# Gate and up of a gated feed-forward block: rows stationary, 512 weight columns moving, results staged in pairs and turned by transfers

## The chip, the cores and the metric

The kernel runs on one core of one Trainium2 chip. The metric is device time in microseconds for one execution. "Before" has three runs: 1088.67, 1089.22 and 1090.31 us, median 1089.22. A separate execution was profiled.

## The reference

One transformer block on x of 2048 rows by 1024 columns, bf16: a layer norm, attention with 32 query heads that share one key head and one value head of width 32, a residual, a second layer norm, and a feed-forward of width 3584 whose gate is a sigmoid.

```python
q = (x @ wq).reshape(B, S, H, Dh)            # 32 heads of 32
k = x @ wk; v = x @ wv                       # one head of 32
scores = einsum("bhqd,bkd->bhqk", q, k) * (Dh ** -0.5)
o = einsum("bhqk,bkd->bhqd", softmax(scores), v)
h = x + (o reshaped to S x 1024) @ wo        # x in the products above is layernorm(x)
g, u = layernorm(h) @ w_gate, layernorm(h) @ w_up      # 1024 -> 3584
h2 = h + (sigmoid(g) * u) @ w_down                     # 3584 -> 1024
```

## The kernel before

The 2048 rows are 16 row tiles of 128 (t); two tiles are a unit, 8 units in all (UNITS). Attention works in 512 *bursts*. A burst is 128 keys against 128 rows of one tile and 16 heads: four matmuls of 32 contraction rows side by side (s_burst, L871, out S_ps), then two exponentials on ACT of 128x1024 (one_exp, L891, mostly into the ring Pr). A tile has 32 bursts. DVE adds pairs of exponentials for the row sums (L928, L940). PE multiplies them by V (pv_group, L978) and by ones (sum_group, L1025 and L1040), DVE normalises (L1083), and the attention output takes the place of the queries in QT. Then follow the output product with wo (wo_group), the second norm (stats2), and a transfer that transposes the normalised rows of the tile into QT again (transpose2, L623).

The feed-forward of a unit follows. gate_group and up_group compute 512 results a row per PSUM bank in the same helper (mm, L373; L375 where a matmul is issued in four narrow pieces of 32 output columns, so that it has the form of the PV product beside it). Weights are the stationary operand: 128 of their columns, with the transposed rows of the unit moving past them, 256 of them, or 128 where only the first tile of the unit is ready. So the result stands with the feed-forward width on partitions, as the down product needs it. ACT makes a tanh of the gate (L1305, into gu; the sigmoid is half of tanh plus one), DVE multiplies (L1327, into hact), and down_group reads hact as its stationary operand and writes rows out (L1365, then a transfer).

Weights of gate and up come in loads of 512 KB, 128 partitions x 8 x 256 columns (load_halves), issued on SP's queue into slots: four in wgu, the parts of QT that finished units leave free, and at the end the ring Pr. SP's queue also carries x, the outputs and the transposing transfers. Where a unit's second tile is not ready, its first runs alone (first_tile), and the weights of that step are loaded again for the second unless they are held.

The order of everything is fixed when the program is built. A planner keeps a clock for each engine and a price for each kind of work (T_MM, T_EXP, a price for changing the form of matmul, the rate of transfers) and deals the instructions out: a burst when its PSUM banks should be free, otherwise PV work by PV_PLAN, otherwise products of queries, wo, gate, up or down that its clocks say are ready (halves_ready, rows_ready). A PE with nothing ready gets dummy matmuls (fill, L409).

Of the kernel before, what the change touches and what calls it, by code (L numbers as in the profile page):

```python
# [7 lines left out]
BF16 = mybir.dt.bfloat16  # L8
# [78 lines left out]
def bass_sequential_preLN__grouped_kv_mqa__glu_gated_glu__prompt_kernel(  # L87
# [32 lines left out]
    U_PLAN = "75601517"  # L120
    PV_PLAN = "bbabdaaaEabeEaBadddabaEaAaaABaBabBaBbaEaaBAAaBabaaaBaDaaabaDabaabaEedEEa"
    WO_PLAN = "aababaaa"
    PV_HOLD = 0
    BANK_WAIT = 0.1
    NPB = 4
    G_SUM, HCH, HB0 = 4, 4, 2
    LN_LEAD = 4
    LN_RATE = 0.35
    T_PLAN = "aaaddadd"
    H_ROOM = 0.2  # L130
    Q_PLAN = "dadddddddddaddddddddddaddddddddd"
    SUM_PLAN = "ppppdddp"
    HOLD0 = 2
    K_BUSY = 10
    TODO = ["v5", "Q2", "q1b", "q1a", "k2", "v3", "q1d", "q0c", "C1", "v0", "C3", "v6", "v2", "v4", "C2", "v7",
            "k3", "v1", "q0d", "k1", "q1c"]
# [17 lines left out]
    WD_FROM, WD_GAP, WD_LATE = 30, 6, 14  # L154
    WD_GAP2 = 1
    TURN = 2
# [3 lines left out]
    QREC = 24  # L160
    QORD = 0
    URG0 = 0
    K_ACT = 3
    T_MM, T_FIX, T_SW, T_EXP, T_TANH, T_ADD = 0.0004167, 0.00267, 0.0995, 0.91, 0.479, 0.61
# [4 lines left out]
    with ExitStack() as es:  # L169
# [6 lines left out]
        QT = sb("QT", [NQ, S])  # L176
# [42 lines left out]
        d_sl = [ctr(f"d_sl{i}") for i in range(25)]  # L219
        block = EC(nc.Block())  # L220
# [37 lines left out]
        halves += [QT[:, :, c[0] * P:(c[1] + 1) * P] for c in UNITS[:-1]]  # L258
# [10 lines left out]
        def _(unused):  # L269
            sp, pe, act, dve, pool = nc.sync, nc.tensor, nc.scalar, nc.vector, nc.gpsimd  # L270

            def dma(q, dst, src, c, kb=256):
                q.dma_start(dst, src).then_inc(c.sem, 16)
                c.n += 16
                begin = max(CLK[id(q)][0], k_dma[0])
                k_dma[0] = begin + kb / (140.0 if q is pool else 275.0)
                c.at[c.n] = k_dma[0] + 1.15 + kb * 0.0037
                return (c, c.n)
# [77 lines left out]
            I_US, I_MAX = 4.0, 180  # L356
# [203 lines left out]
            def pe_transpose(t):  # L560

                need(pe, xn_val[t], ident_val)
# [181 lines left out]
            def q_tile(t, qs, on_act=False):  # L744
                items, n = [], len(qs)
                for h, q in enumerate(qs):
                    items += mm_list([(wq[:, q // 2, dt, q % 2 * P:(q % 2 + 1) * P], xnT[:, t // TPQ, dt, t % TPQ * P:(t % TPQ + 1) * P])
                                      for dt in range(DT)], lambda bank, h=h: bank[:, h * P:(h + 1) * P], P)

                def evac(bank, tick):  # L750
                    out = QT[:, qs[0]:qs[0] + n, t * P:(t + 1) * P]
# [11 lines left out]
                return _Group(items, evac, [wq_need(q) for q in qs] + xnT_ready(t))  # L763
# [8 lines left out]
            def q_group(q, c0, n):  # L772
                def evac(bank, tick):
# [5 lines left out]
                    out, src = QT[:, q, c0:c0 + n], bank[:, 0:n]  # L779
# [19 lines left out]
            def q_rows(g):  # L799
                t, i = ORDER[g]  # L800
                return QT[:, i // 2 * 4:i // 2 * 4 + 4, t * P:(t + 1) * P]

# [42 lines left out]
            def p_tile(k, h):  # L845
                kind, i = place[k]
                if kind == "Q":
                    c0 = (i + 4) * QC
                    return QT[:, 4 * h:4 * h + 4, c0:c0 + QC]
# [12 lines left out]
            def s_burst(k):  # L862
# [7 lines left out]
                for j in range(4):  # L870
                    ins = pe.matmul(S_ps[:, ((2 * k + j // 2) % 3) * 2 + j % 2, :],  # L871
                                    lhsT=kT4[DH * j:DH * (j + 1), kt * P:(kt + 1) * P],
                                    rhs=QT[DH * j:DH * (j + 1), i // 2 * 4:i // 2 * 4 + 4, t * P:(t + 1) * P],
# [94 lines left out]
            def pv_group(n):  # L968
# [3 lines left out]
                for b in bs:  # L972
                    def f2(bank, b=b):
# [7 lines left out]
                        if summed(g):  # L981
                            pv_done[0] = use(kx) + 1
                            return c_pv.inc(ins, 0.218, 0.17)
                        if b == bs[-1]:
                            return c_pe.inc(ins, 0.218, 0.17)
                        k_pe[0] += 0.218
                    items.append((0.218, f2, lambda k_=BURST_NO[g, b]: p_time(k_)))
# [17 lines left out]
            def sum_group(n):  # L1005
# [15 lines left out]
                def fs(bank):  # L1021
# [6 lines left out]
                    r = c_pe.inc(ins, 0.218, 0.17)  # L1028
# [4 lines left out]
                if not plain:  # L1033
                    items.append((0.218, fs, sum_time))
                alone = [BURST_NO[g, b] for b in bs] if plain else range(NB - 2, NB) if final else []
                for n, kx in enumerate(alone):
                    def fd(bank, n=n, kx=kx):
# [6 lines left out]
                        if plain:  # L1044
                            pv_done[0] = use(kx) + 1
                            return c_pv.inc(ins, 0.218, 0.17)
                        return c_pe.inc(ins, 0.218, 0.17)
                    items.append((0.218, fd, lambda kx=kx: p_time(kx)))

                def evac(bank, tick):  # L1050
                    if head and x % 2 == 0:
# [91 lines left out]
            down_last, gu_last = {}, {}  # L1143
            st2_val, h_done = {}, set()

            def wo_group(t, dc):
# [10 lines left out]
                items = mm_list([(QT[:, q, t * P:(t + 1) * P], wo[:, q, dc * 512:(dc + 1) * 512])  # L1157
# [623 lines left out]
```

## Time and profile before

| | us |
|---|---|
| median of the runs | 1089.22 (1088.67 to 1090.31) |
| the profiled execution's own time | 1089.49 |
| its span, first to last instruction | 1087.8 |
| PE busy | 1069.5 |
| ACT busy | 1001.9 |
| DVE busy | 896.4 |
| granted TensorE clock | 1.00 throughout |

A row of the page reads: line, engine, operation, out<-in by the program's names, shapes, count, then busy time and mean ns of one, then idle time of the engine before them and what ended it. Matmuls overlap, so a mean of 273 ns for one of 256 columns is its way through the array, and the time it costs is read from start to start. A row of the timeline merges like instructions: start, from the first start to the last end, and xN of them.

### The profile page before, as it was taken

To read this page: it belongs to the slowest core of one execution; us is meant where nothing else is said; L and a number is where in the kernel's file an instruction comes from. 1 tells how busy PE (TensorE), PEld (TensorE's weight loads), DVE (VectorE), ACT (ScalarE), POOL (GpSimd) and SP (SyncE) were. 2 spreads that over 40 slices of the span, in tenths; PEclk is the share of its full clock that TensorE was granted. 3 is DMA by queue.
4 is the path that set the end of the run, shared out by engine and by line. 5 is a ranking of instruction groups with operands and counts; after the bars stand their busy time and mean duration, and the time that the engine had idled before them with its cause. 6 is when DMAs were issued, how large, how long until landed. Compare 5 with 4: busy or idle time off the path is not lost.

```text
span 1087.8 us, 31948 instructions
## 1 busy us (share of the span) xinstructions
PE 1069.5 (98%) x13878; PEld 612.5 (56%) x13930; DVE 896.4 (82%) x1481; ACT 1001.9 (92%) x1151; POOL 64.0 (6%) x135
## 2 busy tenths in 40 slices
PE   8999999999999999999999999999999999999999
PEld 7433366544665456643666356653665447653884
DVE  7879898799798888888988988799988999798321
ACT  6999999999999999999999999999999999999110
POOL 2422110000000000000000000000000000000000
PEclk9999999999999999999999999999999999999999
DMA  8657338832977458770976619770686509771660
GB/s 199 132 123 213 90 111 231 240 89 70 230 206 169 117 138 226 213 188 26 248 203 182 136 32 276 196 179 26 158 227 185 126 22 261 203 191 41 152 175 20
DMA packets 320268, 169.98 MB, mean 156 GB/s; under 512 B 39424, under 2 KB 314112, under 8 KB 320128
## 3 DMA queue, kind: packets, MB, share of 16 engines
q1 hardware_dynamic: 315312, 158.23, 56.7%
q0 software_dynamic: 2592, 9.44, 2.6%
q8 instruction: 110, 1.80, 0.7%
q10 hardware_dynamic: 2224, 0.26, 0.2%
q14 instruction: 30, 0.25, 0.1%
HBM read 155.84 MB, written 4.19 MB: 147 GB/s over the span
## 4 chain that ended last, share of the span: by engine, by line
PE 66%; ACT 4%; issue 1%; DVE 1%; ACTq 0%
PE X_ps L373 40%; PE S_ps L871 10%; PE X_ps L375 8%; PE X_ps L978 7%; ACT Pr L891 3%; PE X_ps L1025 1%; ACT gu L1305 1%; DVE pairs L928 0%; DVE pairs L940 0%; DVE olp L994 0%; DVE hact L1327 0%; PE X_ps L1040 0%; DVE hx L1365 0%; ACTq L46 0%
## 5 line engine op out<-in xcount | busy, mean ns | idle before, releaser
L891 ACT ACTIVATE Pr<-S_ps 128x1024 bf16<-128x1024 f32 x992 | 941.1, 1181 | 0.4 <-PE S_ps L871 0.3
L928 DVE TENSOR_TENSOR pairs<-Pr 128x1024 bf16<-128x1024 bf16 x470 | 320.0, 682 | 27.4 <-ACT Pr L891 26.8
L940 DVE TENSOR_TENSOR pairs<-pairs 128x1024 bf16<-128x1024 bf16 x408 | 281.6, 690 | 12.0
L373 PE MATMUL X_ps<-QT,wgu 128*128 128x256 bf16 (+1 forms) x2235 | 215.7, 246 | 0.7 <-DMA QT<-hn 0.7
L871 PE MATMUL S_ps<-QT,kT 32*128 32x512 bf16 x2048 | 202.0, 385 | 2.4 <-ACT Pr L891 1.1
L373 PEld LDWEIGHTS X_ps<-QT,wgu 128*128 128x128 bf16 x2235 | 167.3, 98 | 40.6 <-issue 26.1
L373 PE MATMUL X_ps<-zone,hact 128*128 128x512 bf16 (+2 forms) x650 | 149.4, 371 | 4.4 <-issue 4.0
L373 PE MATMUL X_ps<-QT 128*128 128x128 bf16 (+1 forms) x1550 | 150.3, 246 | 0.0
L871 PEld LDWEIGHTS S_ps<-QT,kT 32*128 32x128 bf16 x2048 | 51.4, 91 | 156.9 <-ACT Pr L891 141.4
L373 PEld LDWEIGHTS X_ps<-QT 128*128 128x128 bf16 x1550 | 115.8, 98 | 25.1 <-issue 16.2
L978 PE MATMUL X_ps<-Pr,V 128*32 128x512 bf16 x1984 | 127.6, 381 | 0.4
L1305 ACT ACTIVATE gu<-X_ps 128x512 f32<-128x512 f32 x112 | 84.7, 756 | 45.8 <-PE X_ps L373 45.8
L1327 DVE SCALAR_TENSOR_TENSOR hact<-gu,X_ps 128x512 bf16<-128x512 f32 x112 | 76.6, 684 | 50.6 <-PE X_ps L373 47.0
L373 PEld LDWEIGHTS X_ps<-zone,hact 128*128 128x128 bf16 x685 | 59.1, 98 | 73.9 <-issue 18.6
L978 PEld LDWEIGHTS X_ps<-Pr,V 128*32 128x32 bf16 x1984 | 46.3, 96 | 51.8 <-issue 13.1
L375 PE MATMUL X_ps<-zone,hact 128*32 128x512 bf16 x956 | 61.9, 380 | 0.0
L464 POOL CAST mean<-mv 128x1 f32<-128x1 bf16 x28 | 7.6, 272 | 822.8 <-DVE mv L1191 791.1
L373 PE MATMUL X_ps<-wo,QT 128*128 128x512 bf16 x208 | 53.5, 380 | 1.3 <-issue 0.6
L373 PE MATMUL X_ps<-zone 128*128 128x128 bf16 (+3 forms) x461 | 49.8, 253 | 2.6 <-DMA zone<-hn 1.1
L375 PE MATMUL X_ps<-QT,wgu 128*32 128x256 bf16 (+1 forms) x1428 | 46.9, 265 | 0.9 <-DVE olp L994 0.9
L1365 DVE SCALAR_TENSOR_TENSOR hx<-X_ps,hx 128x512 bf16<-128x512 f32 (+2 forms) x33 | 22.2, 672 | 25.1 <-PE X_ps L373 23.0
L375 PEld LDWEIGHTS X_ps<-QT,wgu 128*32 128x32 bf16 x1428 | 33.2, 96 | 12.7 <-issue 7.5
(110 smaller groups left out, 631.7 us busy)
## 6 DMA issues: line engine op xcount, KB each, us to landing
wgu<-in_B_w_gate_dram SPq DMA_DIRECT2D x75, 512.0 KB, 5.3
wgu<-in_B_w_up_dram SPq DMA_DIRECT2D x74, 512.0 KB, 5.3
QT<-in_B_w_up_dram SPq DMA_DIRECT2D x49, 512.0 KB, 5.4
QT<-in_B_w_gate_dram SPq DMA_DIRECT2D x48, 512.0 KB, 5.7
zone<-in_B_w_down_dram POOLq DMA_DIRECT2D x14, 512.0 KB, 5.1
hx<-in_A_x_dram SPq DMA_DIRECT2D x17, 256.0 KB, 2.7
out_dram<-hx SPq DMA_DIRECT2D x31, 128.0 KB, 1.7
Pr<-in_B_w_gate_dram SPq DMA_DIRECT2D x5, 512.0 KB, 7.4
```

The costliest lines, as they stand in the source:

```text
L373: return pe.matmul(out, lhsT=lhsT, rhs=rhs, start=start, stop=stop, skip_group_check=main[0])
L375: ins = pe.matmul(out[DH * j:DH * (j + 1)], lhsT=lhsT[:, DH * j:DH * (j + 1)], rhs=rhs, start=start, stop=stop, tile_position=(0, DH * j), ...
L464: return c_pool.inc(pool.tensor_copy(out=mean[:, i:i + 1], in_=mv[:, i:i + 1, 0]), 0.2)
L871: ins = pe.matmul(S_ps[:, ((2 * k + j // 2) % 3) * 2 + j % 2, :], lhsT=kT4[DH * j:DH * (j + 1), kt * P:(kt + 1) * P], rhs=QT[DH * j:DH * ( ...
L891: c_e.inc(act.activation(out=p_tile(k, n % 2), in_=S_ps[:, 2 * pr:2 * pr + 2, :].rearrange("p a (b q) -> p (a b) q", q=QC), func=ACTF.Exp, ...
L928: slot_use[x] = c_dve.inc(dve.tensor_tensor(out=dst(x), in0=p_tile(k - 1, hh), in1=p_tile(k, hh), op=ALU.add), T_ADD, 0.08)
L940: slot_use[x] = slot_use[y] = c_dve.inc(dve.tensor_tensor(out=pairs[:, x, :], in0=pairs[:, x, :], in1=pairs[:, y, :], op=ALU.add), T_ADD, ...
L978: ins = pe.matmul(bank[DH * j:DH * (j + 1), :], lhsT=V[:, kt, :], rhs=p_tile(kx, j // 2)[:, j % 2 * 2:j % 2 * 2 + 2, :], start=b == bs[0], ...
L1025: ins = pe.matmul(bank[DH * j:DH * (j + 1), :], lhsT=ones[:], rhs=pairs[:, sum_wide[(g, j // 2)], j % 2 * 512:(j % 2 + 1) * 512], start=Tr ...
L1305: tanh_val[n] = c_act.inc(act.activation(out=slot, in_=bank, func=ACTF.Tanh, scale=0.5), T_TANH, 0.1)
L1327: gu_read[n] = c_dve.inc(dve.scalar_tensor_tensor(out=hact[:, 2 * fs[0]:2 * fs[0] + ft, r0:r0 + len(ts) * P], in0=slot.rearrange("p (a b) ...
L1365: v = c_dve.inc(dve.scalar_tensor_tensor(out=hv, in0=bank[:, 0:n], scalar=0.5, in1=hv, op0=ALU.mult, op1=ALU.add), 0.03 + n * 0.00113, 0.08)
```

## The change

Gate and up swap their operands. The transposed rows of one tile, 128x128, are now stationary, and 512 weight columns move past them; a step is one tile and 512 columns of gate, then of up. The result now has rows on partitions. DVE writes it as bf16 to one of two staging buffers (the former second half of gu), two steps of 512 columns side by side where they follow one another, and SP issues a transfer that transposes a buffer into hact (send_h). A load still has 512 KB, now 128 partitions x 4 x 512 columns, and is issued only when the load four before it has landed (H_OUT).

QT is stored by unit, [8 units, 8, 256] instead of [8, 2048], so that the queries of a unit are contiguous. The last tile's normalised rows are transposed by eight matmuls into PSUM (transpose2_pe) instead of a transfer. The copy of the key weights moves from DVE to POOL, and the first score burst stands ahead of the second tile's transposes. The planner's prices and plans have new numbers, and the whole order comes out anew.

```diff
-    T_MM, T_FIX, T_SW, T_EXP, T_TANH, T_ADD = 0.0004167, 0.00267, 0.0995, 0.91, 0.479, 0.61
+    T_MM, T_FIX, T_SW, T_EXP, T_TANH, T_ADD = 0.0004167, 0.00267, 0.0985, 0.9165, 0.479, 0.61
-        QT = sb("QT", [NQ, S])
+        QT = sb("QT", [S // QC, NQ, QC])
+        def rows(t):
+            return QT[:, t // TPQ, :, t % TPQ * P:(t % TPQ + 1) * P]
...
             def load_halves():
...
+                    if k_dma[0] > max(k_pe[0], k_sp[0]) + H_LEAD:
+                        return
                     u = half_list.popleft()
                     i, ticks = half_free.popleft()
-                    need(sp, *ticks)
+                    need(sp, *ticks, recent.popleft() if len(recent) == H_OUT else None)
                     _, _, w, f = u
-                    half_val[u] = dma(sp, halves[i], (wu_r if w else wg_r)[:, :, f * 256:(f + 1) * 256], d_sl[i], 512)
+                    src = (wu_r if w else wg_r)[:, f % 2 * 4:f % 2 * 4 + 4, f // 2 * 512:(f // 2 + 1) * 512]
+                    half_val[u] = dma(sp, halves[i].rearrange("p (a e) c -> p a (e c)", e=2), src, d_sl[i], 512, 340.0, 1.6)
...
             def half_items(n, w):
-                for j in range(2 * len(fs)):
-                    for dt in range(DT):
-                            ins = mm(bank[:, j * m:(j + 1) * m], halves[i][:, dt, j % 2 * P:(j % 2 + 1) * P],
-                                     QT[:, dt, r0:r0 + m], dt == 0, dt == DT - 1)
+                for dt in range(DT):
+                        u = us[dt // 4]
+                        ins = mm(bank.rearrange("p (a b) -> p a b", b=256), rows(t)[:, dt, :],
+                                 halves[i][:, dt % 4 * 2:dt % 4 * 2 + 2, :], dt == 0, dt == DT - 1)
...
+            def send_h(now=False):
+                while h_due and (now or when(h_due[0][-1]) <= k_pe[0]):
+                    b, c, t, m, count, tick = h_due.popleft()
+                    tt = t - UNITS[c][0]
+                    need(sp, tick, head_left[0] if c == 0 else down_done[(c - 1, tt)])
+                    d = d_h[b]
+                    sp.dma_start_transpose(hact[:, 4 * m:4 * (m + count), tt * P:(tt + 1) * P],
+                                           stage_h[b][:, 0:512 * count]).then_inc(d.sem, 16)
...
             def up_group(n):
-                    need(dve, tick, tanh_val[n], down_last[c - 1] if c else head_left[0])
-                    gu_read[n] = c_dve.inc(dve.scalar_tensor_tensor(
-                        out=hact[:, 2 * fs[0]:2 * fs[0] + ft, r0:r0 + len(ts) * P], in0=slot.rearrange("p (a b) -> p a b", a=ft),
-                        scalar=1.0, in1=bank.rearrange("p (a b) -> p a b", a=ft), op0=ALU.add, op1=ALU.mult), 0.61, 0.08)
+                    need(dve, tick, tanh_val[n], None if pair else h_free[b])
+                    i = len(pair)
+                    gu_read[n] = v = c_dve.inc(dve.scalar_tensor_tensor(
+                        out=stage_h[b][:, 512 * i:512 * (i + 1)], in0=slot, scalar=1.0, in1=bank, op0=ALU.add, op1=ALU.mult),
+                        0.61, 0.08)
...
             def down_group(c, tt, dc, lo=0, n=512):
-                        need(pe, hact_val[(t, f1)])
+                        need(pe, hact_val[(t, ft // 4)])
...
-            need(dve, wk_val)
-            wk4_val = c_dve.inc(dve.tensor_copy(out=wk4.rearrange("p a (r j) -> p a r j", r=4),
+            need(pool, wk_val)
+            wk4_val = c_pool.inc(pool.tensor_copy(out=wk4.rearrange("p a (r j) -> p a r j", r=4),
...
             run_group(q_tile(0, [2, 3], True))
+            s_burst(0)
+            exps(0, (0,))
+            exps(0, (1,), False)
+            k[0] = 1
             f0, f1 = pe_transpose(1)
```

How the order moves, at three places. First PE in the middle of the program, before: six bursts (L871) with gate and up between them (names with wgu or QT; 32x256 is four narrow pieces).

```order
L871 MATMUL S_ps<-QT,kT 128x512 x4
L375 MATMUL X_ps<-QT,wgu 32x256 x40
L373 MATMUL X_ps<-QT,wgu 128x256 x2
L871 MATMUL S_ps<-QT,kT 128x512 x4
L1025 MATMUL X_ps<-pairs,ones 32x512 x4
L375 MATMUL X_ps<-QT,wgu 32x256 x12
L373 MATMUL X_ps<-QT,wgu 128x256 x11
L871 MATMUL S_ps<-QT,kT 128x512 x4
L373 MATMUL X_ps<-QT,wgu 128x256 x14
L373 MATMUL X_ps<-QT 128x256 x3
```

And the same bursts in the change, where the score burst is L888 and the helper's lines are L382 and L384:

```order
L888 MATMUL S_ps<-QT,kT 128x512 x4
L1042 MATMUL X_ps<-pairs,ones 32x512 x4
L384 MATMUL X_ps<-wgu,QT 32x512 x24
L888 MATMUL S_ps<-QT,kT 128x512 x4
L382 MATMUL X_ps<-wgu,QT 128x512 x3
L382 MATMUL X_ps<-QT 128x512 x3
L888 MATMUL S_ps<-QT,kT 128x512 x4
L382 MATMUL X_ps<-QT 128x512 x5
L382 MATMUL X_ps<-wgu,QT 128x512 x2
```

Gate and up have half as many matmuls between two bursts, each of 512 columns. Second, SP while the last unit's weights are loaded, in the change (in the order before, SP has two transposes for a whole unit, those of the normalised rows):

```order
L1382 DMA_TRANSPOSE hact<-gu 128x8x128
L282 DMA QT<-in_B_w_up_dram 128x4x512 x2
L282 DMA QT<-in_B_w_gate_dram 128x4x512 x2
L282 DMA wgu<-in_B_w_up_dram 128x4x512
L1382 DMA_TRANSPOSE hact<-gu 128x8x128
L282 DMA wgu<-in_B_w_up_dram 128x4x512
```

The transposes of staged results stand between the loads, on one queue with them. Third, PE behind the last score burst, before:

```order
L373 MATMUL X_ps<-zone,hact 128x512 x8
L373 MATMUL X_ps<-QT 128x128 x16
L373 MATMUL X_ps<-QT,wgu 128x128 x16
L373 MATMUL X_ps<-wo,QT 128x512 x16
L373 MATMUL X_ps<-QT 128x128 x16
```

and in the change:

```order
L1057 MATMUL X_ps<-Pr,ones 32x512 x8
L382 MATMUL X_ps<-QT 128x512 x8
L382 MATMUL X_ps<-kT,QT 128x512 x4
L382 MATMUL X_ps<-QT 128x512 x4
L382 MATMUL X_ps<-wo,QT 128x512 x16
```

Before, a down product of the unit ahead (zone,hact) still stood there and the first gate of the last unit followed it in narrow matmuls; now that down product is done earlier, and gate and up of the last unit run there at once.

More of the change, by code (lines that the diff above doesn't have):

```diff
@@ L748, in q_tile, with f @@
                                       for dt in range(DT)], lambda bank, h=h: bank[:, h * P:(h + 1) * P], P)
+                for i in range(DT if parts else 0):
+                    def f(bank, i=i, f1=items[i][1]):
+                        need(pe, parts[i // 2])
+                        return f1(bank)
+                    items[i] = (items[i][0], f)
                 def evac(bank, tick):
-                    out = QT[:, qs[0]:qs[0] + n, t * P:(t + 1) * P]
+                    out = rows(t)[:, qs[0]:qs[0] + n, :]
                     src = bank[:, 0:n * P].rearrange("p (a b) -> p a b", a=n)
@@ L1421, in rows_ready @@
             def rows_ready(ts, now):
[L1422 removed]
+                return all(t in hnT_val and when(hnT_val[t], hnT2_val.get(t)) <= now for t in ts)
             def halves_ready(us, now):
```

291 lines of the change are left out of this document (194 added, 97 removed).

## The prediction

> **What bounds the kernel now.** I read the page first (who is busy, and which shapes), then the stretches of the span, then the order of time around the last exponential.
>
> ```profile
> PE 1069.5 (98%) x13878; PEld 612.5 (56%) x13930; DVE 896.4 (82%) x1481; ACT 1001.9 (92%) x1151; POOL 64.0 (6%) x135
> L891 ACT ACTIVATE Pr<-S_ps 128x1024 bf16<-128x1024 f32 x992 | 941.1, 1181 | 0.4 <-PE S_ps L871 0.3
> 400.00:500.00 100.00, 99.09 (x1299) 58.64 (x1301) 89.29 (x144) 100.00 (x117) 2.12 (x4) 1.00 0.73 192
> 900.00:1000.00 100.00, 99.37 (x1297) 57.85 (x1300) 87.87 (x140) 99.95 (x116) 2.12 (x4) 1.00 0.68 180
> 1000.00:1088.00 88.00, 85.30 (x913) 64.17 (x916) 22.55 (x37) 12.75 (x19) 1.29 (x3) 1.00 0.45 115
> 994.18 10.21 ACT L891 ACTIVATE Pr<-S_ps 128x1024 bf16<-128x1024 f32 x11
> 1001.88 0.40 PE L871 MATMUL S_ps<-QT,kT 32*128 32x512 bf16 x4
> ```
>
> Each stretch row gives PE, PEld, DVE, ACT, POOL busy, then the granted clock (1.00), the DMA share and GB/s. Two engines are full at once. ACT runs the exponentials without a hole (0.4 us idle before 992 of them) and is done at 994.18 + 10.21 = 1004.4; PE is 99% busy beside it and alone after it. So the span is a stretch that ACT paces, up to the last score burst at 1001.88, and a PE tail of 1087.8 - 1001.9 = 85.9 us. Work that PE sheds in the first part only counts if tail work moves up into it.
>
> **Prices.**
>
> ```profile
> 434.04 2.03 PE L373 MATMUL X_ps<-QT,wgu 128*128 128x256 bf16 x17
> 436.00 0.40 PE L871 MATMUL S_ps<-QT,kT 32*128 32x512 bf16 x4
> 436.33 1.49 PE L373 MATMUL X_ps<-QT,wgu 128*128 128x256 bf16 x12
> 998.53 1.68 PE L373 MATMUL X_ps<-zone,hact 128*128 128x512 bf16 x7
> 1000.14 0.40 PE L871 MATMUL S_ps<-QT,kT 32*128 32x512 bf16 x4
> 1013.62 1.06 PE L373 MATMUL X_ps<-QT 128*128 128x128 bf16 x16
> 1014.51 1.06 PE L373 MATMUL X_ps<-QT,wgu 128*128 128x128 bf16 x16
> ```
>
> From start to start: sixteen narrow matmuls take 0.89 us, 56 ns each. The three prices fit columns / 2.4 + 2.7 ns: 56 for 128, 109.4 for 256, 216 for 512. Seventeen of 256 then take 1.86 of the 1.96 us, and seven of 512 take 1.51 of 1.61: the 0.10 left is the change to the four-row form of a score burst. Back is the same (436.00 to 436.33 is 0.216 for the burst and 0.11).
>
> [...]
>
> **The change, part by part.** *Gate and up.* By the programs' order they are now 2,496 matmul steps of 256 columns and 2,176 of 128 (four narrow pieces issued together count as one step): 2,496 x 0.1094 + 2,176 x 0.056 = 394.9 us. The change has 1,792 of 512: 387.1. That is -7.8: the same columns, 2,880 fixed parts of 2.7 ns fewer.
>
> *Order dealt anew.* Changes of form on PE fall from 1,062 to 1,035: -2.7. Added on PE: 16 dummy matmuls more (61 instead of 45), 8 that transpose the last tile, and 128 more query matmuls for the same columns: 0.9 + 0.45 + 0.35 = +1.7. PE's own work in all: -8.8.
>
> *Where it lies.* Summed after the last burst, PE has 83.3 us of matmuls before and 67.5 after, -15.8; up to that burst it has 7.0 us more. So the new order moves tail work under the exponentials. ACT's list up to the last exponential is the same but for 101 tanh instead of 98, at 0.47 each:
>
> ```profile
> 440.97 0.79 ACT L1305 ACTIVATE gu<-X_ps 128x512 f32<-128x512 f32 x1
> 441.44 1.23 ACT L891 ACTIVATE Pr<-S_ps 128x1024 bf16<-128x1024 f32 x1
> 11.76 0.62 PE L566 MATMUL S_ps<-pairs,zone 128*128 128x128 bf16 x8 [0.26 <-DVE zone L533]
> 12.31 0.39 PE L871 MATMUL S_ps<-QT,kT 32*128 32x512 bf16 x4
> ```
>
> that is +1.4. The first burst no longer stands behind the second tile's transposes (the last two rows: 0.55 between their starts and 0.26 of waiting): 0 to -0.8. Against that the copy of the key weights goes to POOL, which no row prices for this size, and the key product waits for it; I take -0.5 in all.
>
> If ACT alone sets the last burst, the end moves by +1.4 - 15.8 = -14.4. If PE sets it, by -8.8. Which one? Up to 1001.9 PE had 974.4 us of priced work, so 27.5 us were start, waits and small losses. After, 981.4 + 27.5 = 1008.9, against 1003.3 that ACT needs: PE is late unless it loses 5.6 us less. PE's idle time is 1087.8 - 1069.5 = 18.3 us in all, some of it waits for ACT, which go away once PE is the later one; and there are 3,500 matmuls fewer to lose a few ns on. I take -4 of the 5.6 (bounds 0 and 5.6). Before the transfers: -8.8 - 4 - 0.5 = -13.3.
>
> *Transfers.* The order has 356 loads of 512 KB of gate and up weights instead of 260: a unit's first tile now often runs alone and its weights are read again for the second. To these come 67 transposes of staged results on the same SP queue.
>
> ```profile
> wgu<-in_B_w_gate_dram SPq DMA_DIRECT2D x75, 512.0 KB, 5.3
> DMA packets 5701, 2.82 MB, mean 282 GB/s; under 512 B 388, under 2 KB 5699, under 8 KB 5699
> L623 SPq DMA_TRANSPOSE QT<-hn x16: 1237/1496/5252, 133.0 to 1017.5; - x16
> DMA to landing us min/median/max: 3.0/3.6/7.9
> PEld X_ps L373 <- DMA QT<-hn: 0.9, 1, 0.9
> ```
>
> The second row is a stretch (278 to 288 us) with loads queued one behind another: 282 GB/s, 1.86 us a load. The next two are the transposes of normalised rows (ns on SP at least, median and most; then us to landing): behind queued loads one held SP for 5.25 us and landed after 7.9. A unit takes 124 us (64 bursts); its 44.5 loads and 8.4 transposes need 44.5 x 1.86 + 8.4 x 1.5 = 95 us of it, so they fit on average. In the half of a unit with most gate and up work, some 33 loads and 6 transposes need 70 us of 62; 5 to 10 loads (9 to 19 us) can be there beforehand. So it fits, with little room. Lower bound 0: the last row is the largest wait of PE for a transfer after the first 30 us, and none is for weights. Upper bound: 2 us in each of 7 units, 14. I take +2.5, near the lower end, since loads are issued ahead and the lines read are now 1 KB instead of 512 B. [...] No row here reads weights in 1 KB lines.
>
> *Staging.* DVE's gate-times-up product now goes to one of two staging buffers and waits until that buffer was turned. Behind it on DVE stand the pair sums that feed PE and free the exponentials' ring. With both tiles in step a buffer comes round after two steps; a step is 16 matmuls, 3.46 us in the tail and about 5.5 beside attention, so 6.9 us at least against 3.6 (median) to 7.9: hidden, except for a late one in the tail. At the very end the previous tile's down product, 56 x 0.216 = 12.1 us, covers the last turns. Bounds 0 and 4; I take +1. Contiguous queries by unit change no count and no width of score matmuls: 0.
>
> Sum: -13.3 + 2.5 + 1 = -9.8 on the profiled execution's 1089.49 us, which is 0.27 above the median of the runs: 1089.22 - 9.8 = **1079.4**.
>
> **The rivals.** *ACT keeps the pace* (PE absorbs the 7 us and the transfers cost nothing): -14.4 - 0.5 gives 1074.3. For it: ACT had no holes before. Against: PE is to be filled beyond what it did in that stretch before. Chance 0.18.
>
> *The weight reads become the bound*, the slower side. Where a first tile runs alone, four matmuls (0.86 us) use up a load; with some 65% of PE's time for such work that is a load every 1.33 us against 1.86. Over 28 such loads in a unit the queue falls 15 us behind, its 6 transposes add 9, and 9 to 19 are covered: 5 to 15 us are left, if the order does not put other work there. It decides from 12.3 / 7 = 1.8 us lost in each unit after the first; at 3 us the time is 1089.2 - 12.3 + 21 = 1098. For it: the 70 us in 62. Against: no wait for weights before, and down products can stand between. Chance 0.12.
>
> *Waits of 11 to 14 us* from both causes eat the gain: about 1089. Chance 0.05. A fifth of a per cent, 2.2 us, is about what a measurement of this kernel can tell from no change.
>
> **How the numbers follow.** The forecast has 0.65 (its own range 1076 to 1085). Faster 0.65 + 0.18 = 0.83, same 0.05, slower 0.12. The range runs from just under the ACT case to the point where the gain is gone: 1073.5 to 1090, which leaves out most of the slower rival and little else.
>
> **What would show it.** Gate and up as 512-column matmuls at 216 ns; the last burst at 1003 to 1007 and a tail of 70 to 73 us behind it. ACT with a few us of waits for score bursts would say that PE sets the end, none that ACT does. Waits of PE for weight loads of more than 5 us in all, or of DVE's staging product for its transposes, would say that the transfers were priced too low; then, or if the last burst came after 1012, the forecast is wrong.

## The result: slower by 1.7%

| us | before | change |
|---|---|---|
| median of 5 runs on the same chip | 1089.69 (1088.67 to 1090.63) | 1108.53 (1105.41 to 1110.22) |
| the profiled execution: span | 1087.8 | 1104.7 |
| start of the last score burst | 1001.88 | 1031.05 |
| from there to the end of the span | 85.9 | 73.7 |
| granted TensorE clock, mean | 1.00 | 0.998 |

The ratio is 1.0168, with a 95% interval of 1.0147 to 1.0189. The forecast was 1079.4 in a range of 1073.5 to 1090: the direction is wrong. The tail became 12.2 us shorter, as the forecast had it; the part ahead of it became 29.2 us longer.

The page of the changed kernel: busy engines, then the exponentials and the two largest groups of gate and up (busy, mean ns of one | idle time ahead of them and what ended it), then the loads of gate weights into wgu and QT (count, KB, us from issue to landing), and from the timeline the first and the last score burst (start us, us).

```profile
PE 1058.1 (96%) x10338; PEld 423.7 (38%) x10440; DVE 900.5 (82%) x1491; ACT 1010.2 (91%) x1152; POOL 64.2 (6%) x136
L908 ACT ACTIVATE Pr<-S_ps 128x1024 bf16<-128x1024 f32 x992 | 935.3, 1069 | 19.5 <-PE S_ps L888 17.7
L382 PE MATMUL X_ps<-wgu,QT 128*128 128x512 bf16 x744 | 191.5, 382 | 12.0 <-DMA wgu<-in_B_w_gate_dram 4.0
L382 PE MATMUL X_ps<-QT 128*128 128x512 bf16 x515 | 134.8, 382 | 12.8 <-DMA QT<-in_B_w_up_dram 3.5
wgu<-in_B_w_gate_dram SPq DMA_DIRECT2D x96, 512.0 KB, 6.1
QT<-in_B_w_gate_dram SPq DMA_DIRECT2D x75, 512.0 KB, 6.1
11.24 0.40 PE L888 MATMUL S_ps<-QT,kT 32*128 32x512 bf16 x4 [0.56 <-ACT QT L770]
1031.05 0.39 PE L888 MATMUL S_ps<-QT,kT 32*128 32x512 bf16 x4
```

Gate and up now wait for their weights, which they never did before, and ACT, which had waited 0.4 us ahead of its 992 exponentials, waits 19.5 us for score bursts that come late. A load lands 6.1 us after its issue (median; 5.3 before).

The waits of the changed kernel (engine, line, what it waited for: us in total, times, longest):

```profile
ACT Pr L908 <- PE S_ps L888: 17.7, 28, 2.2
DVE gu L1417 <- DMA hact<-gu: 13.8, 3, 7.0
PEld X_ps L382 <- DMA wgu<-in_B_w_gate_dram: 6.3, 6, 2.3
PEld X_ps L382 <- DMA wgu<-in_B_w_up_dram: 5.6, 8, 1.1
PEld X_ps L382 <- DMA QT<-in_B_w_up_dram: 5.2, 8, 1.5
```

With the rows of the other slots (QT and Pr, gate and up, L382 and L384), PE's weight loader stood 25.1 us for gate and up weights, in 35 waits of which the longest is 2.35 us. Before it was 0. Below, "waits for weights" is this sum. Part of it lies beside matmuls that still run: PE itself stood idle for weights for 14.5 us.

The same stretches as before (us; PE, PEld, DVE, ACT, POOL busy with counts; clock, DMA share, GB/s), and the tail:

```profile
400.00:500.00 100.00, 96.45 (x880) 36.14 (x891) 86.30 (x139) 97.35 (x111) 3.50 (x7) 1.00 0.86 241
900.00:1000.00 100.00, 96.88 (x911) 36.19 (x922) 84.31 (x136) 98.41 (x113) 3.40 (x7) 1.00 1.06 289
1031.00:1105.00 74.00, 68.54 (x390) 32.04 (x392) 17.97 (x30) 9.24 (x15) 1.30 (x3) 1.00 0.64 178
```

In each hundred PE lost about 2.5 us and ACT 2.7 and 1.5, and nowhere much at once. (Of PE's matmuls 11 records are missing in each of the two stretches, 880 against 891 weight loads, so its share is rough.) In the second stretch DMA moves 289 GB/s where it moved 180.

How one such wait looks in the chain (start us, us, what):

```profile
637.56 6.68 DMA wgu<-in_B_w_up_dram
644.25 0.14 issue
644.38 3.44 PE X_ps L382 x8
647.82 0.33 PE S_ps L888 x4
```

A load is issued at 637.56 and lands 6.7 us later; gate or up starts with it at once, and a score burst, and so ACT, stands behind that. The eight matmuls take 3.44 us here, twice their price of 8 x 0.216 = 1.73; the granted clock was 0.51 from 644.20 to 647.60 (last section).

### The profile page after: what moved, and what is told of

It is laid out like the page before. It is cut to its first block, busy times and chain, and to the rows that moved or that the text cites. A ratio compares the mean times of both kernels' runs of the same rounds, so it can differ in the third digit from the quotient of the medians.

```text
span 1104.7 us, 25471 instructions
## 1 busy us (share of the span) xinstructions
PE 1058.1 (96%) x10338; PEld 423.7 (38%) x10440; DVE 900.5 (82%) x1491; ACT 1010.2 (91%) x1152; POOL 64.2 (6%) x136
## 4 chain that ended last, share of the span: by engine, by line
PE 72%; DMA 12%; ACT 8%; DVE 4%; issue 4%; POOL 0%; SPq 0%; ACTq 0%; DVEq 0%
PE X_ps L382 40%; PE S_ps L888 11%; PE X_ps L384 10%; PE X_ps L995 8%; ACT Pr L908 6%; DMA wgu<-in_B_w_up_dram 5%; DMA QT<-in_B_w_gate_dram 2%; DMA wgu<-in_B_w_gate_dram 1%; DMA hact<-gu 1%; DMA QT<-in_B_w_up_dram 1%; DVE pairs L945 1%; ACT wo L908 1%; DVE pairs L957 1%; DMA QT<-hn 1%; ACT gu L1357 1%
## 5 line engine op out<-in xcount | busy, mean ns | idle before, releaser
L908 ACT ACTIVATE Pr<-S_ps 128x1024 bf16<-128x1024 f32 x992 | 935.3, 1069 | 19.5 <-PE S_ps L888 17.7
L888 PE MATMUL S_ps<-QT,kT 32*128 32x512 bf16 x2048 | 202.0, 385 | 6.5 <-ACT Pr L908 2.6
L382 PE MATMUL X_ps<-wgu,QT 128*128 128x512 bf16 x744 | 191.5, 382 | 12.0 <-DMA wgu<-in_B_w_gate_dram 4.0
L382 PE MATMUL X_ps<-zone,hact 128*128 128x512 bf16 (+2 forms) x688 | 160.2, 371 | 4.1 <-issue 3.2
L382 PE MATMUL X_ps<-QT 128*128 128x512 bf16 x515 | 134.8, 382 | 12.8 <-DMA QT<-in_B_w_up_dram 3.5
L888 PEld LDWEIGHTS S_ps<-QT,kT 32*128 32x128 bf16 x2048 | 51.5, 91 | 212.7 <-ACT Pr L908 194.2
L1417 DVE SCALAR_TENSOR_TENSOR gu<-gu,X_ps 128x512 bf16<-128x512 f32 x112 | 76.7, 685 | 63.0 <-PE X_ps L382 40.7
L382 PEld LDWEIGHTS X_ps<-wgu,QT 128*128 128x128 bf16 x777 | 67.4, 98 | 103.9 <-issue 23.1
L1357 ACT ACTIVATE gu<-X_ps 128x512 f32<-128x512 f32 x112 | 71.0, 634 | 38.0 <-PE X_ps L382 37.7
L382 PEld LDWEIGHTS X_ps<-zone,hact 128*128 128x128 bf16 x720 | 62.3, 98 | 79.7 <-issue 19.7
L382 PEld LDWEIGHTS X_ps<-QT 128*128 128x128 bf16 x547 | 47.5, 98 | 75.8 <-issue 16.4
L382 PE MATMUL X_ps<-wo,QT 128*128 128x512 bf16 x239 | 58.9, 380 | 0.2 <-issue 0.2
L384 PE MATMUL X_ps<-wgu,QT 128*32 128x512 bf16 x844 | 55.9, 381 | 0.6 <-DMA wgu<-in_B_w_gate_dram 0.5
L384 PE MATMUL X_ps<-zone,hact 128*32 128x512 bf16 x816 | 51.7, 380 | 0.0
L382 PE MATMUL X_ps<-zone 128*128 128x128 bf16 (+3 forms) x548 | 49.5, 238 | 1.7 <-DVE QT L772 0.7
L384 PE MATMUL X_ps<-QT 128*32 128x512 bf16 x580 | 39.6, 380 | 1.5 <-DMA QT<-in_B_w_gate_dram 1.5
```

The costliest lines, as they stand in the source:

```text
L382: return pe.matmul(out, lhsT=lhsT, rhs=rhs, start=start, stop=stop, skip_group_check=main[0])
L384: ins = pe.matmul(out[DH * j:DH * (j + 1)], lhsT=lhsT[:, DH * j:DH * (j + 1)], rhs=rhs, start=start, stop=stop, tile_position=(0, DH * j), ...
L908: c_e.inc(act.activation(out=p_tile(k, n % 2), in_=S_ps[:, 2 * pr:2 * pr + 2, :].rearrange("p a (b q) -> p (a b) q", q=QC), func=ACTF.Exp, ...
L1357: tanh_val[n] = c_act.inc(act.activation(out=slot, in_=bank, func=ACTF.Tanh, scale=0.5), T_TANH, 0.1)
L1417: gu_read[n] = v = c_dve.inc(dve.scalar_tensor_tensor(out=stage_h[b][:, 512 * i:512 * (i + 1)], in0=slot, scalar=1.0, in1=bank, op0=ALU.ad ...
```

## The experiments

The first five and the ninth keep the order of the change's instructions. The kernel before, run beside each, had 1088.8 to 1089.2 us.

**1. Half of each load.** All loads of gate and up (but four into the zone) bring half of their rows; gate and up are then computed from stale weights in part.

```diff
+ n_ = 2 if i <= H_KT else 4
- dma(sp, halves[i].rearrange(...), src, d_sl[i], 512, ...)
+ dma(sp, halves[i].rearrange(...)[:, 0:n_, :], src[:, 0:n_, :], d_sl[i], 512, ...)
```

> Same order as the change, but every load of gate and up weights brings only the first half of its rows (256 KB instead of 512; the four loads into the former projection area stay whole), so the products are not those of the reference. Transfer theory (PE waits because weights come late): the waits for weights go, the last score burst comes at 1003 to 1010 instead of 1031 and the time is 1077 to 1085. Rival (the order itself holds PE and ACT up, since there is no slack between them and PE's pieces are 216 ns long): the weights matter little and the time stays above 1098.

Measured: 1083.39 us, ratio 0.9949 (0.9926 to 0.9971), span 1081.0. Waits for weights 0.7 us; the last burst at 1009.7. The first row below is the exponentials' group, the second the loads:

```profile
L908 ACT ACTIVATE Pr<-S_ps 128x1024 bf16<-128x1024 f32 x992 | 934.7, 1093 | 4.0 <-PE S_ps L888 2.6
wgu<-in_B_w_gate_dram SPq DMA_DIRECT2D x96, 256.0 KB, 3.2
```

Only the weight loads differ between this run and the change, so they account for the 25.1 us between the two (1108.53 - 1083.39). With data that arrive in time, the change is faster than the kernel before.

**2. A quarter of each second read.** The 132 loads that bring a step's weights again for the second tile of a unit bring a quarter.

```diff
+ n_ = 1 if u[1] else 4        # u[1]: loaded again
```

> Same order; only the 132 loads that fetch weights a second time for a unit's second tile bring a quarter of their rows (the rest of the slot keeps old data, so the result is not the reference's). Transfer theory with the second reads as the cause: they are 28% of the traffic, most of the lateness goes: 1080 to 1090, last burst at 1004 to 1013. If the transposes on the queue are the cause instead: 1098 or more. If neither: no change from 1105 to 1110.

Measured: 1103.93 us, ratio 1.0138 (1.0109 to 1.0168); waits for weights 24.2 us. 28% of the weight data are gone, and 4.6 us of the time. The second reads, to which the prediction put the added loads, are not the main cause. The exponentials' row is nearly that of the change:

```profile
L908 ACT ACTIVATE Pr<-S_ps 128x1024 bf16<-128x1024 f32 x992 | 933.9, 1071 | 19.1 <-PE S_ps L888 17.7
```

**3. Turns of one block.** A turn is a transfer that transposes a staging buffer into hact. From the second unit on, each of them moves 128 columns instead of 512 or 1024; the down product reads stale data in part.

```diff
- sp.dma_start_transpose(hact[:, 4 * m:4 * (m + count), ...], stage_h[b][:, 0:512 * count])
+ n_ = 1 if c else 4 * count
+ sp.dma_start_transpose(hact[:, 4 * m:4 * m + n_, ...], stage_h[b][:, 0:128 * n_])
```

> Same order; from the second unit on a transposing transfer turns one block of 128 columns instead of four or eight (hact keeps old values elsewhere, so the result is not the reference's). It stays one instruction on the queue in the same place. If the data of the turns holds the weights up: 1090 to 1098. If their place on the queue or the second reads do: within 4 us of the change, 1103 to 1110.

Measured: 1103.88 us, ratio 1.0138 (1.0097 to 1.0178); waits for weights 23.3 us, DVE's for turns 9.9 instead of 13.8. Another 4.6 us, not the main cause. It is no cost on top of the weights' either: with the loads cut as well, in the ninth experiment, the time is only 0.6 us under that of the first.

**4. No wait for the load four before.** SP issues a load as soon as its slot is free; nothing of the computation is left out.

```diff
- need(sp, *ticks, recent.popleft() if len(recent) == H_OUT else None)
+ if len(recent) == H_OUT:
+     k_sp[0] = max(k_sp[0], when(recent.popleft()))     # the planner's clock alone
+ need(sp, *ticks)
```

> Same order; the wait of a weight load for the landing of the fourth load before it is left out on SP (the planner still reckons with it). Nothing is left out of the result. If this wait leaves the transfer engines idle between loads: 1098 to 1104, and SP's 106 us of waits for landings are gone. If the engines are simply full, or weights wait for slots, the queue only grows longer, turns land later and the time is the same or worse: 1105 to 1115.

Measured: 1107.02 us, ratio 1.0167 (1.0137 to 1.0196). The loads go out earlier and queue longer (median 6.5 us to landing, against 6.1 after the first 40), and nothing is gained: the limiting wait is not at the issue.

**5. Half of each first read.** The counterpart of the second: the first reads bring half, the second reads all.

```diff
+ n_ = 4 if u[1] or i > H_KT else 2
```

> Order of the change kept. Every first read of a gate or up weight tile (220 of them, the four that go to the zone excepted) brings half of its rows, so the products of gate and up are computed from stale rows in part; the 132 second reads come whole. That takes away 110 loads' worth of data, about as much as the 99 that the second reads gave up before for 4.6 us. Theory A (each load lands later than the written order has it: 3.9 us after its issue when nothing is queued, 6.0 in the middle, 0.7 us more than planned on average, and the first reads are those that PE needs at once): with half the data the first reads land in 3.0 to 4 us, PE's waits for weights fall from 19 us to under 5, time 1083 to 1090. Theory B (the amount of data: each load taken out is worth the same, wherever it is): 4.6 us x 110 / 99 = 5 us, time 1103, waits for weights of 12 us and more.

Measured: 1086.90 us, ratio 0.9979 (0.9968 to 0.9990), span 1085.0; waits for weights 3.2 us. Two rows of its page:

```profile
L908 ACT ACTIVATE Pr<-S_ps 128x1024 bf16<-128x1024 f32 x992 | 935.1, 1089 | 7.0 <-PE S_ps L888 5.2
wgu<-in_B_w_gate_dram SPq DMA_DIRECT2D x60, 256.0 KB, 3.4
```

As much data as in the second experiment (110 loads' worth against 99), and 21.6 us instead of 4.6: theory A's number, not B's. What counts is when the first reads land, not how much is moved. The two parts, 21.6 and 4.6, add up to the 25.1 of the first experiment within the error (the second reads were cut to a quarter in the second experiment, to half in the first).

That can be followed in the written order. The planner has a time for each load on its own clock; set against the trace, loads land 0.7 us later after their issue than it took (mean after the first 40), the first reads 0.8 (median) to 2.5 (one in twenty). It is not the rate that it took wrongly: queued loads land every 1.5 us, as it had them (340 GB/s). It is what follows a transfer, 2.4 us for 1.6: a load alone lands 3.9 us after its issue (median of 8). On the planner's clock a quarter of the first reads is used within 2.0 us of the planned landing; in the kernel before, that quarter reaches to 6.3 us. PE waits, all engines are late by that, and since the order leaves neither PE nor ACT idle, the lag is not made up. The trace's time of a load's issue less the planner's, us (median of the loads and turns within 12 us of each place):

| planned at | 157 | 308 | 457 | 664 | 808 | 1030 |
|---|---|---|---|---|---|---|
| change | 0.1 | 2.8 | 6.3 | 13.2 | 18.5 | 24.8 |
| half of each load (1) | 0.3 | 0.2 | 0.7 | 0.4 | 0.5 | 1.1 |

The change's own clock ends at 1077.6 us, the span at 1104.7. For the kernel before these are 1080.9 and 1087.8. On paper the change was the faster one.

**6. The planner told of the later landing.** One number of its bookkeeping is changed (a load lands 2.4 us after its transfer; alone, that makes the 3.9 us after its issue that the trace shows, where the change took 3.1). A new order follows; the computation is whole.

```diff
- dma(..., 512, 340.0, 1.6)
+ dma(..., 512, 340.0, 2.4)
```

> One number of the order's bookkeeping changed, nothing of the computation: a load of gate or up weights is taken to land 2.4 us after its transfer instead of 1.6 (alone: 3.9 us after its issue, as measured, instead of 3.1). The order that comes out has 316 loads instead of 356, 180 dummy matmuls instead of 61, PE work of 1053.5 us instead of 1046.8, and its own clock ends at 1093.9 instead of 1077.6. Theory A (loads later than planned): the order that knows it loses little beyond its own clock; the run with half of each load ended 3.4 us after the clock, so a span of 1096 to 1101 and a time of 1098 to 1103, PE's waits for weights under 6 us. Theory B (too much data for the queue): 11 per cent fewer loads take 11 per cent of the waits, and the 6.7 us of dummies come on top: span above 1108, waits for weights near 17 us.

Measured: 1112.56 us, ratio 1.0213 (1.0183 to 1.0243), span 1110.7. Each theory is half right: waits for weights fell to 8.4 us, nearer to A's 6 than to B's 17 (which started from 19 us, where the sum used here has 25.1), but the run ended 16.8 us behind its own clock, where A had 2 to 7, and the span is B's. The timeline shows one place where the rest came from (start, us, queue or engine, line, what, count, idle before):

```profile
1048.71 2.66 SPq L1382 DMA_TRANSPOSE hact<-gu  x1
1051.47 0.53 SPq L282 DMA_DIRECT2D QT<-in_B_w_up_dram  x1
1052.05 11.79 SPq L1382 DMA_TRANSPOSE hact<-gu  x2
1057.15 0.69 DVE L1417 SCALAR_TENSOR_TENSOR gu<-gu,X_ps 128x512 bf16<-128x512 f32 x1 [10.18 <-DMA hact<-gu]
1058.59 5.68 PE L382 MATMUL X_ps<-Pr,QT 128*128 128x512 bf16 x19 [4.57 <-ACT gu L1357]
```

A turn behind queued loads is late, DVE's next staging product waits 10.2 us for the buffer, ACT's tanh for DVE, PE for ACT: 4.6 us at one place. DVE waited 28.5 us for turns in four such places, where the change had 13.8. Over all, queued turns landed about 1.2 us later than the planner took and held SP up to 4.3 us where it took 1.25.

**7. All transfers at their measured prices, tables searched anew.** Loads as in 6, turns 1.2 us later and dearer for SP; the planner's tables (the order of PV pieces, of query and wo groups, some bounds) were searched anew for the earliest end of its own clock under these prices. Two bounds are new among them: how far a product may be dealt ahead of the planned landing of its weights (H_MARGIN), and how many steps of a unit may stand with the first tile done alone (F_MAX). The computation is whole.

```diff
- dma(..., 512, 340.0, 1.6)
+ dma(..., 512, 335.0, 2.4)
- k_sp[0] += 1.25
+ k_sp[0] += 1.25 + (1.1 if k_dma[0] - k_sp[0] > 1.2 else 0.0)
- k_dma[0] = max(k_sp[0], k_dma[0]) + 1.1;  d.at[d.n] = k_dma[0] + (1.5 if queued else 0.9)
+ k_dma[0] = max(k_sp[0], k_dma[0]) + 1.3;  d.at[d.n] = k_dma[0] + (2.3 if queued else 0.8)
- U_PLAN = "07221752"; PV_PLAN = "EAaabCdaAbad..."
+ U_PLAN = "70606502"; PV_PLAN = "DAdEEddDDaDc..."
...
```

> The change's instructions in another order, nothing of the computation left out. The bookkeeping that writes the order takes the landings as the runs showed them (a load 2.4 us after a transfer of 1.53 us, a turn that is queued 1.2 us later than assumed, 1.1 us more of SP for it), and its tables and a few bounds were searched anew under these prices. The order has 260 loads instead of 356, 65 turns, PE work of 1052.9 us (171 dummies), and its own clock ends at 1085.0 us. Theory A (the change lost its time because its order was written for landings that do not come): the run ends some 3 to 6 us after its clock, as the run with half of each load did, span 1088 to 1091, time 1089.5 to 1093, PE's waits for weights under 5 us and no wait of DVE for a turn above 3 us. Theory C (something else than landings holds the change back, for one the transposes on SP's queue or PE's own losses): the run ends as far behind its clock as the order with the later landings did, 17 us, time above 1103.

Measured: 1099.09 us, ratio 1.0086 (1.0057 to 1.0115), span 1098.1. It is between the two theories: 9.4 us better than the change, still slower than before. Its landings are nearly the planned ones now (over all loads 0.06 us late on average, where the change had 0.6; after the first 40, 0.2 for 0.7; turns 0.14 early), waits for weights are 4.4 us, and both engines are full again. One sign of theory A failed: DVE waited once 6.2 us for a turn, where A had none above 3.

```profile
400.00:500.00 100.00, 98.81 (x884) 36.97 (x885) 88.00 (x142) 99.54 (x116) 3.60 (x7) 1.00 0.86 233
900.00:1000.00 100.00, 99.41 (x874) 36.60 (x872) 88.09 (x143) 99.64 (x116) 4.19 (x9) 1.00 0.70 182
```

But an order that keeps to real landings has 260 loads, 171 dummy matmuls instead of 61, PE work of 1052.9 us instead of 1046.8, and 82.7 us of it behind the last burst instead of 67.5: of what the change had gained on the kernel before (1055.6 and 83.3) little is left. And it ran 13.1 us behind its clock, 6 of these before 220 us, where the new tables also rearranged the head.

**8. The kernel before, half of each load.** The counterpart of the first.

```diff
+ n_ = DT // 2 if i <= H_KT else DT
- dma(sp, halves[i], (wu_r if w else wg_r)[:, :, ...], d_sl[i], 512)
+ dma(sp, halves[i][:, 0:n_, :], (wu_r if w else wg_r)[:, 0:n_, ...], d_sl[i], 512)
```

> The kernel before, in its own order, with every load of gate or up weights (but the four of the zone) bringing half of its rows, so that gate and up are computed from stale rows in part. It is the counterpart of the run in which the change's loads were halved (1083.4). Theory A: the kernel before has no wait of PE for weights after the first 30 us, so it has nothing to gain: 1087 to 1090. If it gains as the change did, 10 us or more, the gain of that run was no matter of the change's loads.

Measured: 1088.75 us, ratio 1.0002 (0.9991 to 1.0013). Its weights were on time; the gain of the first experiment belongs to the change.

**9. The least transfers.** A quarter of each load and turns of one block together, in the change's order (the edits of 1, with 1 for 2, and of 3).

> Order of the change kept. Every load of gate or up weights (but the four of the zone) brings a quarter of its rows, and every turn from the second unit on turns one block of 128 columns, so gate, up and down are computed from stale data in part. It asks what is left when the transfers cost PE next to nothing. Theory D (the rest of the miss is PE's: the 4 us of smaller losses that were counted on do not come, and PE sets the last score burst): the last burst stays at 1008 to 1010, span 1079 to 1082, time 1081 to 1084, hardly under the 1083.4 of the run with half of each load. Theory E (with half of each load, transfers and turns still cost some us): the last burst comes at 1004 to 1006, span 1075 to 1077, time 1077 to 1079, as the forecast without its transfers had it.

Measured: 1082.83 us, ratio 0.9941 (0.9919 to 0.9964), span 1080.9, last burst at 1009.6, no wait for weights. Theory D: what is left of the miss is PE's own.

```profile
L908 ACT ACTIVATE Pr<-S_ps 128x1024 bf16<-128x1024 f32 x992 | 934.3, 1091 | 3.8 <-PE S_ps L888 2.3
900.00:1000.00 100.00, 100.00 (x1022) 37.41 (x1018) 87.23 (x140) 99.56 (x114) 3.73 (x8) 1.00 0.24 65
1009.60:1080.90 71.30, 68.56 (x392) 32.28 (x392) 18.63 (x31) 9.85 (x15) 1.30 (x3) 1.00 0.17 50
```

PE is busy all of these 100 us, and ACT has small holes.

**10. Measured prices, the change's head.** As 7, but the tables that deal the head of the program stay the change's, and only the rest was searched anew. The computation is whole. The lines marked - are those of 7.

```diff
- T_PLAN = "daaadaadddaddddd"; Q_PLAN = "aaaaaddaddddaddd..."; TODO = ["q1b", "C1", "k1", ...]
+ T_PLAN = "aaaaddaddaddddad"; Q_PLAN = "ddaaadddddddaddd..."; TODO = ["q1b", "q3c", "C1", ...]
- U_PLAN = "70606502"; PV_PLAN = "DAdEEddDDaDc..."
+ U_PLAN = "41114610"; PV_PLAN = "EAaabCdaAbdb..."
...
```

> As the order with measured transfer prices (1099.1 us), with the head of the program (norms, queries, keys and values, up to the end of the first four groups) in the change's own order and the other tables searched anew; the computation is whole. 260 loads, 138 dummies, PE work of 1050.8 us, 82.9 us of it behind the last burst, its own clock ends at 1085.7. Theory A (landings, and for that run a head that did not go as planned, make up what it ran behind its clock): 4 to 7 us behind the clock, span 1089.5 to 1093, time 1091 to 1094.5, so within 0.5 per cent of the kernel before and at best a draw. Theory F (orders of this kind run some 13 us behind their clock for a reason that is not in the prices): time 1099 to 1101.

Measured: 1092.21 us, ratio 1.0030 (1.0018 to 1.0041), span 1090.5: 4.8 us behind its clock, as theory A had it. PE waits for no weights at all, and ACT hardly for PE:

```profile
L909 ACT ACTIVATE Pr<-S_ps 128x1024 bf16<-128x1024 f32 x992 | 934.5, 1093 | 1.8 <-PE S_ps L889 1.0
wgu<-in_B_w_gate_dram SPq DMA_DIRECT2D x73, 512.0 KB, 5.0
```

The lag behind the planner is -0.6 us at 157 and 2.3 at 1030; in the seventh experiment it was 3.1 and 10.1. 16.3 us of the change's 19 came back with the computation whole, by another order, which has 96 loads fewer and 77 dummies more. The head is not the only difference from 7: among the bounds searched anew, a load must now have landed 0.3 us before its use on the planner's clock, where the change and 7 let the use be dealt 0.3 us ahead of the landing, and a load waits for the landing of the third ahead of it instead of the fourth. So what the head alone is worth is not shown. The last burst stands at 1005.1 and 85.5 us follow it, about as before. PE's priced work is still 4.8 us below that of the kernel before (1050.8 against 1055.6), with 138 dummies in it against 45; but 39.7 us of the span lie beside it, against 32.2, and what these 7.5 us are is open.

## Why the prediction was wrong, step by step

*What bounds the kernel* was read rightly: two full engines, and a tail. That is also why each late load counted: there is no slack on either.

*Prices of PE.* Right as far as they can be read: in the ninth experiment 512-column matmuls follow one another every 216 ns (median; 217.6 on average), and in the change every 216 (median). That the fewer changes of form brought their part of the 8.8 us rests on the price of 0.10 us each alone; the whole span fell by 6.9 (1087.8 to 1080.9).

*Where it lies.* Right: 85.9 us became 73.7 in the change and 71.3 with the least transfers (70 to 73 said). The first burst starts at 11.24 instead of 12.31 us, 1.1 earlier where 0 to 0.8 was said.

*"I take -4 of the 5.6".* This step failed. In the ninth experiment the span is 34.1 us above PE's priced work (1080.9 - 1046.8); in the kernel before it is 32.2 (1087.8 - 1055.6). Everything PE lost besides priced work grew by 1.9 us where it was to shrink by 4. The last burst at 1009.6 is the 1008.9 that stood in the text ahead of this step: PE set the pace, with all of its old losses. That is 5.9 us of the miss. PE's idle time did fall, from 18.3 to 14.6 us (1080.9 - 1066.3), about as the step had it; but its busy time fell by 3.2 us only (1069.5 to 1066.3), where its priced work fell by 8.8, and what the other 5.6 are is open. The "few ns" on each of 3,500 matmuls were not there to be saved: in the kernel before, matmuls of 128 and 256 columns follow one another every 56.4 and 109.9 ns on average, in all within 2 us of their price. (The 974.4 us of this step do not fit the total used here, 1055.6 - 83.3 = 972.3; in 1008.9, which is 1001.9 + 7.0, the difference cancels.)

*Transfers, +2.5.* This step failed, and it is the larger one: the runs show 25.7 us (1108.53 against 1082.83), turns included, where this term and the next had 3.5. With the 5.9 above that is 28.1 of the 29.1 us by which the forecast missed. Its form was wrong, not only its size. I asked whether a half unit's loads and turns fit into its time, at 1.86 us a load. They do, and a load even took less (1.5 us, last section). But the step took a median over queued loads for the moment at which one lands, and "issued ahead" for cover. The written order left a quarter of the first reads about 2 us of cover at most, on landing times that the diff states (rate 340, 1.6 us) and the trace of before could have been held against. The planner of the kernel before reckoned 4.9 us for a load alone (275 GB/s, and 3.0 us behind the transfer) where its trace has 4.0, so its loads came early; the change reckons 3.1 where the trace has 3.9, so they came late. The bound of "2 us in each of 7 units" had no ground: the change lost 26 us, about 4 in each.

*The slower rival* had the sign, and 1098 for 1108, but another mechanism: a queue that falls 15 us behind where a first tile runs alone. No such backlog shows: 19 of 20 loads landed within 8.2 us of their issue, and within 9.2 in the fourth experiment, where no load is held back for the fourth ahead of it. Many small waits, not a few long ones, stand behind the loss (35 of them, the longest 2.35 us).

*Staging, +1* (0 to 4). The third experiment has 4.6 us for the data of the turns, but of that only 0.6 is left where the loads are cut as well, so it seems to act by way of the weights. The step took 3.6 us (median) for a turn, from the transposes of the kernel before; turns behind loads took 6.2 (median). It held them hidden but for one in the tail, and two of the three places where DVE waits 13.8 us for them lie in the middle, at 693 and 822 us (4.6 and 7.0).

*What would show it.* The text named waits for weights above 5 us, DVE's waits for turns and a last burst after 1012 as the signs that transfers were priced too low. They were 25.1 us (14.5 of it with PE idle), 13.8 us and 1031.

So: the change as a whole, the swap and the order dealt for it, is worth 6.4 us (0.6%) when weights are at hand (1082.83 against 1089.23); no run tells the swap alone. They were not at hand: the order was built on landings 0.7 us too early, and where it is built on real ones the order is not the same, and the gain is gone. The better of the two orders dealt on them ends at 1092.2, 0.3% behind the kernel before. Whether an order exists that keeps the 6.4 us as well is open; neither the seventh nor the tenth experiment is one.

## What to carry to other kernels

With two engines full (PE 96% and ACT 91% busy), the transfers cost this kernel not their share of bandwidth, but the time by which they landed after the moment of use: PE's weight loader waited 25.1 us for them, and 25.1 us came back with half of each load (experiment 1). Where two engines are full, compare the landing that a written order assumes with the one in the trace, load by load, before trusting its clock. Where volume is suspected, take the same amount of data from loads of two kinds: here first reads held 21.6 us and second reads 4.6. And an order dealt under optimistic prices can lean on just the places where they are optimistic: with one number, the landing, put right and nothing else, the planner dealt 316 loads instead of 356 (experiment 6).

## What the runs showed of the hardware

Loads with lines of 1 KB came faster than loads with lines of 512 B, at about 350 against 295 GB/s. Within a stretch of queued loads the slices of the DMA row (GB/s) of the kernel before, with 512 B a line, and of the change, with 1 KB, are (278 to 288 us and 636 to 662 us, 40 slices each):

```profile
GB/s 349 312 281 303 299 295 293 283 244 264 303 287 301 295 301 295 295 287 295 297 287 291 293 287 289 295 289 291 291 307 258 305 293 297 297 291 205 131 158 229
GB/s 33 87 321 369 265 329 326 358 331 350 341 232 99 22 101 335 332 350 348 351 348 342 350 348 227 63 184 380 255 227 288 323 359 355 317 265 260 343 355 215
```

In these stretches queued loads landed 1.8 us apart before and 1.5 in the change: the loads with 1 KB came a fifth faster. No run changed the line length alone.

In the changed kernel the granted clock fell once to half, for 3.41 us, after a short wait: PE waited 2.05 us for a gate load up to 642.86 us, and the clock fell at 644.15. A wait as long, 2.26 us for DVE up to 822.63, had no fall behind it (first the two waits, then the stretches around the fall):

```profile
642.86 1.04 PE L382 MATMUL X_ps<-wgu,QT 128*128 128x512 bf16 x3 [2.05 <-DMA wgu<-in_B_w_gate_dram]
822.63 0.39 PE L382 MATMUL X_ps<-QT 128*128 128x512 bf16 x1 [2.26 <-DVE gu L1417]
640.00:644.00 4.00, 1.89 (x13) 0.61 (x13) 2.44 (x4) 2.54 (x4) 0.00 (x0) 1.00 1.44 314
644.20:647.60 3.40, 3.24 (x12) 0.99 (x8) 0.69 (x1) 2.16 (x3) 0.00 (x0) 0.51 0.81 211
647.80:652.00 4.20, 4.20 (x72) 1.58 (x74) 3.88 (x7) 3.82 (x5) 0.00 (x0) 1.00 1.09 349
```

8 matmuls took 3.44 us, twice their price of 1.73: the fall cost some 1.7 us beyond the wait itself. The mean of 0.998 for the span is this stretch alone (3.41 us at half in 1104.7), and the loss of the change does not hang on it: the run that gives the median of 1108.53 us has a mean clock of 1.000.

The trace's own record of the clock sets the two waits apart. It has the clock at full from 5.85 to 644.15 us, which is 187 times 3.413, then at half for 3.413 us, then at full again to the end of the span. Cut from 5.85 us on into windows of 3.413 us, PE was idle for 2.11 us in sum in the window that ends at the fall, and for at most 1.37 in any other. The wait up to 822.63 lies across a border at 821.64, with 1.28 us on one side and 0.99 on the other. Before, the clock did not fall in the span, and cut in the same way PE was idle for at most 1.11 us in a window. This reading fits one fall in two traces; what idle time brings a fall is not shown.
